# A linear-attention block with a feed-forward part on one core: w_ch1 in pieces of whole rows, one pair of half-rows instead of two, another order of the steps

## The chip, the cores and the metric

The kernel runs on one core of a Trainium2 chip. The metric is the device time of one execution in microseconds; lower is better. A core has five engines with queues of their own: TensorE (PE, with its weight loads as PEld), VectorE (DVE), ScalarE (ACT), GpSimd (POOL) and SyncE (SP, which here only issues DMAs). All wait for each other through semaphores.

## The reference

Two parts follow each other. The first is a recurrent linear attention for 4 batches, 8 heads, 768 tokens and 48 channels a head; the second is a layer norm and a two-layer feed-forward part with a residual.

```python
for t in range(S):                                  # S = 768, state is [B, H, 48, 48]
    cur = einsum('bhd,bhe->bhde', u[None] * kt, vt)
    y[:, :, t] = einsum('bhd,bhde->bhe', rt, state + cur)
    state = w[None, :, :, None] * state + einsum('bhd,bhe->bhde', kt, vt)
x = y.transpose(0, 2, 1, 3).reshape(B, S, 384)
xn = (x - mean(x)) / sqrt(var(x) + 1e-6) * g_ln
out = x + maximum(xn @ w_ch1, 0) @ w_ch2            # w_ch1 is 384 x 1536, w_ch2 is 1536 x 384
```

All inputs and the output are fp32.

## The kernel before, in words

The tokens are cut into 24 chunks of 128 (six for each batch). Two neighbouring chunks are one attention group, 12 in all. For the feed-forward part the chunks are grouped again by `GROUPS`: eight single chunks, six groups of two, four single ones.

Every step is a small function with a short name, and `PLAN` is a long list of entries "name,number,engine" that are issued in this order. `v`, `s` and `g` mean VectorE, ScalarE and GpSimd; `-` means that the step has only one engine (TensorE, or SyncE for a load or store). Nothing reorders the steps afterwards: each engine's queue holds its own steps in the order of the list. So PLAN fixes which engine does a product or a copy, and what stands behind what.

The steps that matter here:

- `LK`, `LR`, `LV` load k, r and v of one chunk; a packet is one head's row of 48 numbers. `LK2`, `LR2`, `LV2` load a pair of chunks so that a partition holds two neighbouring tokens, and a packet is 96 numbers. r is loaded as pairs for groups 0 to 8 in both versions. k and v are loaded as pairs only for the first `PAIRS` groups.
- `SKH`/`SK2`/`SK` and `SRH`/`SR2`/`SR` multiply k and r by powers of w into bf16 (`sk`, `sr`): a product of two tensors in on-chip memory. `CV2` casts v to bf16 (`vv`). `VB2` multiplies v by a number per head (`Vb`), `Q2` multiplies the transposed k and r, `ZD` scales the state.
- `TRk`/`TRr` transpose sk and sr on TensorE and `TCk`/`TCr` copy them out; from group 4 on sk (and from group 9 on sr) is transposed by a DMA instead (`TDk`, `TDr`).
- `AT`/`AM`, `S`/`ZU`, `Y`/`X` are the attention itself: scores and their mask, the state, the output with the v term. `AT2`, `AM2`, `Y2` are the same for chunks held as pairs.
- `XN`, `SQ`, `RS` are the norm; `LT`/`XT` (TensorE and a copy) or `LTD` (DMA) transpose its result.
- `LW1` loads a piece of w_ch1, `SW` scales one 128 x 512 block of it by g_ln into bf16, in blocks i = 3n + kc for columns n and rows kc; `IW2` loads a third of w_ch2 from GpSimd's queue. `UP` is a feed-forward block of the first layer, `RL` its relu, `DN` a third of the second layer of a chunk, `OT` scaling and residual, `STO` the store.
- `DU` issues matmuls of 512 columns on a tile of zeros, as often as its number divided by 512.

A w_ch1 piece before is a third of the columns of all rows, `w1_f[n]` (128 x 3 x 512, packets of 2 KB). The UP entry number is 16 times the group plus the block m, which for a single chunk covers columns n = m: UP,2 needs SW,6 to 8, UP,17 (group 1, m = 1) needs SW,3 to 5, UP,0 needs SW,0 to 2.

In traces several steps share one line, since a helper records them: products of two tensors have line 205, copies line 200 (ScalarE) or 202. They are told apart by their tiles.

## Time and profile before

| what | value |
|---|---|
| timed runs | 147.73, 149.15, 152.63 us (median 149.15) |
| profiled execution, span from first to last instruction | 147.5 us; what lies around the span is not on the page, and the fastest timed run is 0.2 us longer |
| busy PE, PEld, DVE, ACT, POOL | 141.5, 111.1, 112.3, 82.4, 72.0 us |
| granted TensorE clock | 1.000 |
| DMA | 27.18 MB in 85097 packets, 80338 of them under 512 B |
| loads of k, r, v (issue to landing) | 4.2 to 5.0 us |
| w_ch1, three pieces of 768 KB | 8.6 us |
| w_ch2, three pieces, issued by GpSimd | 6.0 us |

The page gives the busy time of each engine, the span in 40 slices with the busy share in tenths, the DMA queues, the chain of waits that ended last, and the costliest groups of instructions. A row of a timeline has start, duration, engine, line, operation, output and inputs, shapes and, in brackets, the idle time ahead of it with what ended it. A row of a table of waits has the sum, the number and the longest of them.

### The profile page before, as it was taken

The numbers are of one execution on the slowest core, as the hardware profiler recorded it, in microseconds if no ns is written. First come the engines' busy times: TensorE is split into PE (matmuls) and PEld (weight loads), VectorE is DVE, ScalarE is ACT, GpSimd is POOL, SyncE is SP. The second block draws the span as 40 slices with busy tenths as digits, with TensorE's granted clock in tenths as the row PEclk, the third lists the DMA queues.
The fourth block names the chain that finished last, engine by engine and source line by source line (L and its number), as shares of the span: only waits on it lengthen the run. The fifth ranks groups of instructions, "written<-read, shape, count | busy, mean of one in ns | idle before, by whom it ended". The sixth has DMA issues, their size and how long they took to land.

```text
span 147.5 us, 4689 instructions
## 1 busy us (share of the span) xinstructions
PE 141.5 (96%) x1943; PEld 111.1 (75%) x1943; DVE 112.3 (76%) x206; ACT 82.4 (56%) x181; POOL 72.0 (49%) x96
## 2 busy tenths in 40 slices
PE   7899999799999999999999999999999999999991
PEld 3375767699987788787778787778877777878881
DVE  3499999889559887998989999499644886851642
ACT  4657783986977737736766543115795164537010
POOL 7507687984070475794854194627129330614000
PEclk9999999999999999999999999999999999999999
DMA  4999997999959899999899997998959894213023
GB/s 112 300 242 240 192 339 187 283 243 215 220 95 231 202 225 165 264 205 258 164 192 196 195 235 124 173 204 227 197 112 191 182 142 154 82 46 119 8 99 111
DMA packets 85097, 27.18 MB, mean 184 GB/s; under 512 B 80338, under 2 KB 83540, under 8 KB 85076
## 3 DMA queue, kind: packets, MB, share of 16 engines
q1 hardware_dynamic: 84642, 25.70, 78.3%
q0 software_dynamic: 432, 1.18, 4.3%
q8 instruction: 15, 0.25, 0.7%
q14 instruction: 6, 0.05, 0.1%
q10 hardware_dynamic: 2, 0.00, 0.0%
HBM read 18.88 MB, written 4.72 MB: 160 GB/s over the span
## 4 chain that ended last, share of the span: by engine, by line
PE 65%; SPq 13%; DMA 11%; DVE 6%; POOL 1%; issue 1%; DVEq 0%
PE o L674 28%; PE hp L646 25%; DMA kf<-in_k_dram 6%; DMA w_f<-in_moe_w_ch_dram 5%; SPq L374 4%; SPq L352 3%; PE at L544 3%; PE y L583 2%; SPq L358 2%; PE y L481 2%; PE y L575 2%; SPq L371 1%; SPq L377 1%; DVE hT L664 1%; PE y L460 1%
## 5 line engine op out<-in xcount | busy, mean ns | idle before, releaser
L646 PE MATMUL hp<-xT,w_sb 128*128 128x128 bf16 (+1 forms) x648 | 57.1, 237 | 0.8 <-ACT w_sb L342 0.7
L662 ACT ACTIVATE hT<-hp 128x512 bf16<-128x512 f32 x55 | 32.4, 594 | 40.5 <-PE hp L646 39.7
L646 PEld LDWEIGHTS <-w_sb 128*128 128x128 bf16 x648 | 49.3, 114 | 5.1 <-ACT w_sb L342 1.3
L674 PE MATMUL o<-w_sb,hT 128*128 128x384 bf16 x276 | 53.0, 326 | 0.0
L674 PEld LDWEIGHTS <-hT 128*128 128x128 bf16 x276 | 25.0, 97 | 12.0
L553 DVE TENSOR_TENSOR A<-at,mask 128x1024 bf16<-128x1024 f32 x20 | 24.2, 1216 | 2.1 <-PE at L544 2.1
L492 POOL TENSOR_TENSOR Vb<-vf,cc 128x768 f32<-128x768 f32 x11 | 16.5, 1498 | 14.9 <-ACT cc L200 8.5
L730 DVE SCALAR_TENSOR_TENSOR ot<-o,rs,x 128x384 f32<-128x384 f32 x23 | 14.1, 615 | 12.3 <-PE o L674 7.0
L205 POOL TENSOR_TENSOR sk<-kf,Fk 128x384 bf16<-128x384 f32 x13 | 13.6, 1053 | 8.5 <-DMA kf<-in_k_dram 7.9
L597 ACT ACTIVATE sqj<-x,sm 128x384 bf16<-128x384 f32 x24 | 14.6, 609 | 2.2 <-DVE x L590 2.2
L205 POOL TENSOR_TENSOR Z<-ZS,WLZ 128x384 bf16<-128x384 f32 x8 | 8.0, 1002 | 15.4 <-DVE ZS L565 15.4
L590 DVE SCALAR_TENSOR_TENSOR x<-y,Vb 128x384 f32<-128x384 f32 x20 | 11.0, 552 | 4.5 <-PE y L583 4.1
L664 DVE TENSOR_SCALAR hT<-hp 128x512 bf16<-128x512 f32 x17 | 11.5, 684 | 3.4 <-PE hp L646 3.3
L279 PE MATMUL o<-warm 128*128 128x512 bf16 x33 | 11.3, 427 | 1.0 <-DVE warm L228 1.0
L200 ACT COPY trr<-at 128x512 bf16<-128x512 bf16 (+1 forms) x13 | 9.1, 764 | 4.4 <-PE at L400 4.4
L205 DVE TENSOR_TENSOR sr<-rf,Fr 128x768 bf16<-128x768 f32 (+1 forms) x11 | 9.5, 870 | 1.6 <-DMA rf<-in_r_dram 1.6
L205 POOL TENSOR_TENSOR sr<-rf,Fr 128x384 bf16<-128x384 f32 (+1 forms) x5 | 6.6, 1325 | 7.0 <-DMA rf<-in_r_dram 7.0
L604 ACT ACTIVATE xn<-x,sm 128x384 bf16<-128x384 f32 x13 | 7.8, 609 | 2.3 <-DVE x L590 2.3
L606 POOL TENSOR_SCALAR xn<-x,sm 128x384 bf16<-128x384 f32 x8 | 5.3, 665 | 7.6 <-DVE x L590 7.5
L205 DVE TENSOR_TENSOR q<-trk,trr 128x1024 bf16<-128x1024 bf16 x9 | 7.5, 837 | 1.4 <-ACT xn L604 1.0
L481 PE MATMUL y<-vv,sk 128*128 128x96 bf16 (+1 forms) x96 | 7.3, 204 | 0.3 <-ACT vv L200 0.2
L205 DVE TENSOR_TENSOR sk<-kf,Fk 128x384 bf16<-128x384 f32 (+1 forms) x10 | 7.4, 747 | 0.0
(97 smaller groups left out, 179.4 us busy)
## 6 DMA issues: line engine op xcount, KB each, us to landing
out_dram<-ot SPq DMA_DIRECT2D x23, 192.0 KB, 2.6
kf<-in_k_dram SPq DMA_DIRECT2D x20, 192.0 KB, 4.2
vf<-in_v_dram SPq DMA_DIRECT2D x20, 192.0 KB, 4.3
rf<-in_r_dram SPq DMA_DIRECT2D x9, 384.0 KB, 4.7
...
```

What stands on the lines that cost most here:

```text
L205: engines[e].tensor_tensor(out=out, in0=in0, in1=in1, op=ALU.mult)
L279: nc.tensor.matmul(out=warm_ps[0][:].rearrange("p (a t) -> p a t", a=4), lhsT=warm[:], rhs=rhs, start=True, stop=True)
L481: nc.tensor.matmul(out=t[:, q * E2 : (q + 1) * E2].rearrange("p (e d) -> p e d", e=2), lhsT=lhs, rhs=rhs, start=first, stop=True, skip_gro ...
L492: engines[e].tensor_tensor(out=Vb2(g).rearrange("p (x h d) -> p x h d", x=2, h=H), in0=vals, in1=cc2(g)[:].unsqueeze(3).to_broadcast([P, 2 ...
L553: nc.vector.tensor_tensor(out=AA(i)[:].rearrange("p e q t -> p (e q) t"), in0=psum["at", i][:].rearrange("p e q t -> p (e q) t"), in1=mask ...
L590: nc.vector.scalar_tensor_tensor(out=xx(i)[:], in0=psum["y", i][:, :C], scalar=1.0, in1=Vb(i), op0=ALU.mult, op1=ALU.add, accum_out=sm[i][:],)
L597: nc.scalar.activation(out=sqj[:], in_=xx(i)[:], func=ACT.Square, bias=sm[i][:], scale=-float(C), accum_out=sq[g][:, j : j + 1])
L646: nc.tensor.matmul(out=t[:, a * gw : (a + 1) * gw], lhsT=w1_sb[n][kc][:, fb::FB], rhs=xT(g)[:, :size, kc, :], start=(kc == 0), stop=(kc == ...
L662: nc.scalar.activation(out=o, in_=s, func=ACT.Relu)
L664: nc.vector.tensor_relu(out=o, in_=s)
L674: nc.tensor.matmul(out=psum["o", i][:, :C], lhsT=hT(g)[:, fk, j * P : (j + 1) * P], rhs=w2_sb[d][:, a, :], start=(fk == 0), stop=(fk == FK ...
L730: nc.vector.scalar_tensor_tensor(out=ot(i)[:], in0=psum["o", i][:, :C], scalar=rs[g][:, j : j + 1], in1=xx(i)[:], op0=ALU.mult, op1=ALU.add,)
```

## The change

Four things change. `LW1` loads whole rows: `w1_f[kc]` holds 128 rows of w_ch1 with all 1536 columns (packets of 6 KB), so that the three pieces are cut by rows and each UP needs all three. `PAIRS` goes from 2 to 1, so that group 1 loads k and v as four single chunks (`LK`, `LV` instead of `LK2`, `LV2`) and uses AT, AM, Y instead of AT2, AM2, Y2. On GpSimd `CV2` is a product with two constants instead of a copy. And PLAN is another list: the order differs all through it, and so does the engine of many steps.

```diff
-PAIRS = 2
+PAIRS = 1
 PLAN = """
...
-S,3,- LW1,0,- TCk,2,s DU,512,- SK,6,v LT,1,- Y2,2,- SQ,0,s SW,5,g XT,1,v SW,3,s LV,6,- LT,0,- SW,4,v TRk,3,- Q2,2,g
...
+X,3,v LT,1,- Y,2,- SW,3,s SQ,1,s LK,7,- LK,6,- XT,0,v XT,1,v X,2,v SW,5,v SW,2,v AT,4,- TRr,3,- S,3,- UP,17,- TCr,3,s RL,17,s
...
 """
...
-    w1_f = [const.tile([P, CK, FW], FP32, name=f"w1_f{n}") for n in range(NW)]
+    w1_f = [const.tile([P, F], FP32, name=f"w1_f{kc}") for kc in range(CK)]
...
-    w1_src = moe_w_ch1.rearrange("(kc p) (n f) -> p n kc f", p=P, n=NW)
+    w1_src = moe_w_ch1.rearrange("(kc p) f -> p kc f", p=P)
...
-    def LW1(n, e):
-        nc.sync.dma_start(out=w1_f[n][:], in_=w1_src[:, n])
+    def LW1(kc, e):
+        nc.sync.dma_start(out=w1_f[kc][:], in_=w1_src[:, kc])
...
-        o, s = w1_sb[n][kc][:], w1_f[n][:, kc]
+        o, s = w1_sb[n][kc][:], w1_f[kc][:, n * FW : (n + 1) * FW]
...
     def CV2(g, e):
-        copy(e, vv2(g), vf2(g))
+        if e == "g":
+            nc.gpsimd.tensor_scalar(
+                out=vv2(g), in0=vf2(g), scalar1=1.0, scalar2=1.0, op0=ALU.mult, op1=ALU.mult
+            )
+        else:
+            copy(e, vv2(g), vf2(g))
```

Counted over PLAN, GpSimd gets SK 17 (before 13), SR2 5 (2), SR 4 (3), Q2 4 (3), SW 4 (1), CV2 5 (3), XN 9 (8), RS 9 (8), one SKH and one SRH (0), and fewer VB2, 7 (11), and ZD, 5 (8). VectorE gets VB2 5 (1), ZD 7 (4), XN 6 (3), RL 18 (17) and fewer SK 5 (7, and one SK2), SR2 3 (6), SR 2 (3), SKH and SRH 1 each (2 each), Q2 8 (9), CV2 3 (4), XT 6 (8). ScalarE gets fewer SW, 3 (6), XN, 9 (13), CV2, 4 (5) and RS, 9 (10). The number of zero-tile matmuls stays at 33.

The first place is SyncE's queue between the loads of group 0 and the last piece of w_ch1. The tiles w_f_223 to w_f_225 are the pieces 0 to 2, kf, rf and vf the loaded k, r and v; rf_76 is the r of group 3. Before:

```order
L374 DMA rf_75<-in_r_dram 128x8x96
L352 DMA kf_71<-in_k_dram 128x8x48
L374 DMA rf_76<-in_r_dram 128x8x96
L377 DMA vf_78<-in_v_dram 128x8x96
L352 DMA kf_71<-in_k_dram 128x8x48
L352 DMA kf_72<-in_k_dram 128x8x48 x2
L335 DMA w_f_224<-in_moe_w_ch_dram 128x3x512
L335 DMA w_f_225<-in_moe_w_ch_dram 128x3x512
L358 DMA vf_79<-in_v_dram 128x8x48 x2
L335 DMA w_f_223<-in_moe_w_ch_dram 128x3x512
```

And in the changed kernel:

```order
L376 DMA vf_77<-in_v_dram 128x8x96
L357 DMA vf_78<-in_v_dram 128x8x48 x2
L373 DMA rf_75<-in_r_dram 128x8x96
L334 DMA w_f_224<-in_moe_w_ch_dram 128x1536
L351 DMA kf_71<-in_k_dram 128x8x48
L334 DMA w_f_223<-in_moe_w_ch_dram 128x1536
L373 DMA rf_76<-in_r_dram 128x8x96
L334 DMA w_f_225<-in_moe_w_ch_dram 128x1536
L357 DMA vf_79<-in_v_dram 128x8x48 x2
```

The pieces of w_ch1 moved ahead of the k of chunks 5 to 7 and of the v of group 2 (vf_79); the r of group 3 (rf_76) moved from ahead of all pieces to between the second and the third.

The second place is GpSimd's queue from the products of the first groups to the last load of w_ch2. A tile w_sb_a_b is a scaled block of w_ch1, w_sb_235 to w_sb_237 the thirds of w_ch2; xn is the centred x. Before:

```order
L205 TENSOR_TENSOR sr_87<-rf_75,Fr_209 128x16x48
L492 TENSOR_TENSOR Vb_112<-vf_77,cc_102 128x768
L205 TENSOR_TENSOR sk_84<-kf_71,Fk 128x8x48 x2
L205 TENSOR_TENSOR sk_82<-kf_72,Fk 128x8x48
L606 TENSOR_SCALAR xn_126<-x_114,sm_141 128x384
L492 TENSOR_TENSOR Vb_113<-vf_78,cc_103 128x768
L346 TENSOR_SCALAR w_sb_2_231<-w_f_224,g_neg 128x512
L205 TENSOR_TENSOR q_97<-trk_93,trr_96 128x1024
L606 TENSOR_SCALAR xn_128<-x_116,sm_143 128x384
L349 DMA w_sb_235<-in_moe_w_ch_dram 128x1536
```

And in the changed kernel, from the Q2 of group 1 on:

```order
L204 TENSOR_TENSOR q_98<-trk_92,trr_95 128x1024
L204 TENSOR_TENSOR sk_84<-kf_71,Fk 128x8x48
L348 DMA w_sb_235<-in_moe_w_ch_dram 128x1536
L610 TENSOR_SCALAR xn_127<-x_115,sm_142 128x384
L204 TENSOR_TENSOR sr_85<-rf_76,Fr_209 128x16x48
L348 DMA w_sb_236<-in_moe_w_ch_dram 128x1536
L345 TENSOR_SCALAR w_sb_1_227<-w_f_224,g_neg 128x512
L345 TENSOR_SCALAR w_sb_0_226<-w_f_223,g_neg 128x512
L348 DMA w_sb_237<-in_moe_w_ch_dram 128x1536
L345 TENSOR_SCALAR w_sb_1_233<-w_f_224,g_neg 128x512
L345 TENSOR_SCALAR w_sb_2_234<-w_f_225,g_neg 128x512
```

The first load of w_ch2 moved ahead of the scalings of w_ch1; the product of group 3's r (sr_85 from rf_76), which VectorE did before, stands ahead of two scalings that UP,0 reads (w_sb_1_227 and w_sb_0_226).

More of the change, by code (lines that the diff above doesn't have):

```diff
@@ L66 @@
-SB,23,- OA,23,v SA,23,-
+WF,0,s TL,0,s ML,0,v LN,0,s MI2,0,g MM,0,g MP,5,g MO,0,v MZ,0,v MP,2,g MP,0,g MM2,0,g MI,0,g MP,4,g MP,1,g MW,0,v DU,3072,-
+WBM,0,- LK2,0,- FK2,1,s FK2,0,s SKH,0,g SKH,1,v LR2,0,- LK,2,- UF,0,- LG,0,- LK,4,- UWR,0,v LR2,1,- LK,3,- LV2,0,- LV,2,- LV,3,-
+LR2,2,- LW1,1,- LK,5,- LW1,0,- LR2,3,- LW1,2,- LV,5,- LV,4,- FR2,1,s FR2,0,s SRH,1,g DU,4608,- TRk,0,- DU,512,- SRH,0,v TCk,0,s
+FK,0,s FR,0,s SR2,1,g SK,3,g MP,3,g TRr,0,- COL,0,- TCr,0,v Q2,0,v UW,0,s CV2,0,g WL,0,s AT2,1,- AT2,0,- DU,3072,- AM2,1,v
@@ new lines @@
+AM2,0,v SK,4,g SK,2,v TRr,1,- S,0,- DU,1536,- TRk,1,- CV2,1,s TCr,1,s TCk,1,s ZU,0,v CC2,0,v VB2,0,g SR2,2,v S,1,- Q2,1,g SK,5,g
+Y2,0,- AT,2,- Y2,1,- TRr,2,- ZU,1,v AM,2,v TCr,2,s X,1,v X,0,v IW2,0,g XN,1,g SR2,3,g IW2,1,g XN,0,s AT,3,- DU,512,- AM,3,v
+S,2,- DU,512,- ZU,2,v CC2,1,s UGC,0,s SW,4,s TRk,2,- DU,1024,- LT,0,- Y,3,- DU,512,- TCk,2,s SW,1,g SW,0,g DU,1536,- VB2,1,v
+X,3,v LT,1,- Y,2,- SW,3,s SQ,1,s LK,7,- LK,6,- XT,0,v XT,1,v X,2,v SW,5,v SW,2,v AT,4,- TRr,3,- S,3,- UP,17,- TCr,3,s RL,17,s
@@ new lines @@
+IW2,2,g UP,0,- AT,5,- UP,1,- Q2,2,v ZU,3,v CV2,2,v AM,5,v RL,0,s SW,6,s UP,16,- S,4,- RL,1,s SQ,2,s SW,7,g SW,8,g XN,2,g UP,2,-
+LT,2,- CC2,2,v ZU,4,v RL,16,s SQ,0,s XN,3,s UP,18,- DN,0,- VB2,2,g XT,2,v RL,2,v RL,18,s LT,3,- AM,4,v UP,34,- Y,5,- X,5,v
+XT,3,v SK,7,g SK,6,g DN,1,- UP,32,- Y,4,- TRk,3,- DN,2,- RS,0,g X,4,v OT,0,v LK,8,- LV,6,- LV,7,- RS,1,g XN,4,g SK,8,v RL,34,s
+TCk,3,s LR2,4,- LK,11,- LK,9,- LV,9,- LR2,5,- SK,9,g LV,8,- LK,10,- TDk,4,- LR2,6,- LV,12,- UP,33,- SQ,3,s AT,6,- AT,7,- CV2,3,s
```

81 lines of the change are left out of this document (35 added, 46 removed).

## The prediction, made before the changed kernel was run

> **What bounds the kernel now.** I read the page's engine line and slices first, then TensorE's own waits, then the start of its long stretch, then the transfers that this start waits for.
>
> ```profile
> PE 141.5 (96%) x1943; PEld 111.1 (75%) x1943; DVE 112.3 (76%) x206; ACT 82.4 (56%) x181; POOL 72.0 (49%) x96
> PE   7899999799999999999999999999999999999991
> ```
>
> TensorE is busy for 96% of the span, VectorE for 76%, GpSimd for 49%. "Busy" says little of the first 27 us, where the program itself issues matmuls on a zero tile (line 279) to fill gaps. So the next question is where the real work becomes dense.
>
> ```profile
> 25.12 0.62 PE L544 MATMUL at<-trr,trk 48*128 48x128 bf16 x16
> 26.10 0.25 PE L646 MATMUL hp<-xT,w_sb 128*128 128x128 bf16 x1
> 26.71 0.25 PE L646 MATMUL hp<-xT,w_sb 128*128 128x128 bf16 x1 [0.37 <-ACT w_sb L342]
> 27.33 1.42 PE L646 MATMUL hp<-xT,w_sb 128*128 128x128 bf16 x22 [0.36 <-ACT w_sb L342]
> 143.74 0.67 PE o L689 x8
> ```
>
> The feed-forward matmuls (UP, line 646) begin at 26.10 and run without a gap from 27.33; the last DN piece ends at 144.4. What waits remain on TensorE in between is the whole answer for 27.4 to 147 us:
>
> ```profile
> PE hp L646 <- ACT w_sb L342: 0.4, 1, 0.4
> PEld L544 <- issue: 1.7, 6, 0.3
> PEld L646 <- ACT w_sb L342: 0.5, 1, 0.5
> PEld L481 <- DVE x L590: 0.5, 1, 0.5
> PEld L646 <- issue: 0.3, 1, 0.3
> PEld L400 <- DVE sr L205: 0.3, 1, 0.3
> ```
>
> The two w_sb rows are the edge of the start. "issue" is no wait for another engine. Only 0.5 + 0.3 us are waits for VectorE. So behind 27.33 lie 117 us in which a better order of VectorE and GpSimd can give back at most 0.8 us, or about 1.5 with some of "issue"; it can lose any amount. What decides is **when the UP stream begins**, and that start waits for w_ch1:
>
> ```profile
> 15.90 7.37 DMA w_f<-in_moe_w_ch_dram
> 19.38 1.00 POOL L205 TENSOR_TENSOR sk<-kf,Fk 128x384 bf16<-128x384 f32 x1 [0.56 <-DMA kf<-in_k_dram]
> 19.57 5.58 SPq L335 DMA_DIRECT2D w_f<-in_moe_w_ch_dram  x1
> 25.32 1.95 ACT L342 ACTIVATE w_sb<-w_f,g_neg 128x512 bf16<-128x512 f32 x3 [1.31 <-DMA w_f<-in_moe_w_ch_dram]
> 2.00:4.00 2.00, 2.00 (x6) 0.93 (x4) 0.14 (x4) 1.06 (x2) 1.82 (x11) 1.00 0.98 249
> 20.00:22.00 2.00, 2.00 (x30) 1.35 (x28) 2.00 (x3) 1.56 (x4) 1.90 (x3) 1.00 1.01 377
> 24.00:26.00 2.00, 2.00 (x59) 1.35 (x57) 2.00 (x6) 0.69 (x3) 2.00 (x2) 1.00 0.48 74
> ```
>
> The first w_ch1 piece lands at 15.90 + 7.37 = 23.3, the second at 25.3 (ACT then scales three blocks, the third of which ends at 27.27 and releases the stream). The third piece sits 5.58 us in SyncE's issue. In the stretch rows the last two numbers are the DMA share and GB/s: the engines are full from 2 us on and half empty at 24 to 26, behind that stuck issue.
>
> **The change part by part.**
>
> *Loads and w_ch1.* Prices first. The last k load before w_ch1 lands at 19.38, so twelve loads (eight pairs of half-rows, four single chunks) took 17.3 us of full engines from 2.0.
>
> ```profile
> DMA packets 2193, 0.55 MB, mean 184 GB/s; under 512 B 2118, under 2 KB 2118, under 8 KB 2193
> q1 hardware_dynamic: 2193, 0.55, 93.4%
> q0 software_dynamic: 432, 1.18, 4.3%
> ```
>
> The first two rows are the stretch 16 to 19, with single chunks of 1024 packets (128 x 8) in it: 0.934 x 3 = 2.80 us, less 0.41 for 75 packets of w_ch1 (0.154 MB at 377 GB/s), is 2.39 us for 2118 packets, so 1.16 us a chunk. A pair is then (17.3 - 4 x 1.16)/8 = 1.58 us. Splitting group 1's k and v from two pairs into four chunks costs 4.64 - 3.16 = 1.5 us of DMA time. A w_ch1 piece is 0.786 MB: 2.1 us at 377 GB/s, or 2.4 (19.3 to 25.3 held two pieces and one v chunk: (6.0 - 1.16)/2). Pieces of whole rows are as large; I take the same 2.1 to 2.4, since the 377 GB/s stretch is the fastest that I see.
>
> In the new order six pairs and six chunks go before the last w_ch1 piece: 2.0 + 6 x 1.58 + 6 x 1.16 + 3 x (2.1 to 2.4) = 24.7 to 25.6. Before GpSimd reaches the head's end it also issues the first w_ch2 load (IW2,0), which was issued at 27.03 and now stands behind SK,5, at about 21 us; the three w_ch2 loads took 4.3% of 147.5, 2.1 us each, so up to 2.1 more: 24.7 to 27.7, taken at 26.5. The 5.58 us in SyncE should mostly go, since three pieces are 384 packets instead of 1152; what is late next is the transfers themselves. Every piece is now needed by every UP, where the old start needed two of three; that eats what the earlier issue wins.
>
> The row with which a rule can be weighed is 377 GB/s with 2 KB rows. The Trainium skill, "DMA: Bandwidth & Descriptors", Specifications, puts the least transfer at line rate at 512 B; by that rule 2 KB and 6 KB rows cost the same and whole rows bring nothing. The trace agrees as far as it goes: by the rule the sum is 24.7 to 25.6 before w_ch2, as above, and no row here shows 6 KB.
>
> *GpSimd's queue before the first UPs.* The r load of group 3 (LR2,3) now stands behind two w_ch1 pieces; it lands one piece before the last, 22.6 to 23.2, up to 25.3 with w_ch2 between, taken at 24.0. GpSimd, in order, waits for it in SR2,3, and behind it stand IW2,1 and the two scalings SW,1 and SW,0, without which UP,0 cannot start.
>
> ```profile
> 12.15 1.81 POOL L205 TENSOR_TENSOR sr<-rf,Fr 128x768 bf16<-128x768 f32 x1 [6.44 <-DMA rf<-in_r_dram]
> 23.37 0.49 DVE L344 TENSOR_SCALAR w_sb<-w_f,g_neg 128x512 bf16<-128x512 f32 x1 [0.18 <-DMA w_f<-in_moe_w_ch_dram]
> 23.44 0.97 POOL L346 TENSOR_SCALAR w_sb<-w_f,g_neg 128x512 bf16<-128x512 f32 x1 [0.94 <-DMA w_f<-in_moe_w_ch_dram]
> 27.03 0.78 POOL L349 DMA_DIRECT2D w_sb<-in_moe_w_ch_dram  x1
> ```
>
> 24.0 + 1.81 + 0.78 + 2 x 0.97 = 28.5 for SW,0 (26.9 to 29.8). UP,17 needs only SW,3, 4 and 5: 26.5 + 0.49 = 27.0, so it runs alone and TensorE then waits for SW,0. Dense work starts at 28.5 instead of 27.33: **+1.2**. Not yet done then, but done in the kernel before: one transpose of sk (TRk,3) and one AT, 0.45 and 0.55 by the rows below: **+1.0**. Done ahead: UP,17, **-0.7**. Two zero-tile matmuls that stood behind 27.33 are gone, 0.2 each: **-0.4**. Sum +1.1.
>
> ```profile
> 28.75 0.38 PE L279 MATMUL o<-warm 128*128 128x512 bf16 x1
> 28.97 0.83 PE L646 MATMUL hp<-xT,w_sb 128*128 128x128 bf16 x12
> 55.71 0.45 PE at L400 x8
> 61.78 0.55 PE at L544 x16
> ```
>
> *Group 1 as single chunks.* AT2 and Y2 on two half-rows become AT and Y. All of it lies before the stream, under the wait for w_ch1, so I cost it at nothing. So too the zeroing of the warm tile, now last of VectorE's memsets (some 1.2 us later), and the halves of SK and SR shared with GpSimd: by the old durations the state of group 0 is some 2 us later, and the first transposed x stands at about 24, with 2.5 us of cover until w_ch1. If that cover goes (w_ch1 at 24.7), up to 0.7 us shows.
>
> *VectorE and GpSimd.* GpSimd gets four SK, one SR, SKH and SRH more (1.0 each, as sk at 19.38), three SR2 and a Q2 (1.8 each), three SW (1.0) and two CV2 (1.3, below), and gives back four VB2 (1.5) and three ZD (about a product of 384, 1.0): 7 + 7.2 + 3 + 2.6 - 9 = 10.8, and 1.4 more as its three old CV2 become slower. So 72 becomes about 84 us. VectorE, which has the other side of most of these, comes out some us lower. Products that coincide do stretch each other:
>
> ```profile
> 21.03 1.48 POOL L492 TENSOR_TENSOR Vb<-vf,cc 128x768 f32<-128x768 f32 x1
> 21.33 1.59 DVE L205 TENSOR_TENSOR sk<-kf,Fk 128x384 bf16<-128x384 f32 x1
> 35.60 0.59 DVE L205 TENSOR_TENSOR sk<-kf,Fk 128x384 bf16<-128x384 f32 x1
> 36.12 0.94 DVE L205 TENSOR_TENSOR sr<-rf,Fr 128x768 bf16<-128x768 f32 x1
> L205 DVE TENSOR_TENSOR sk<-kf,Fk 128x384 bf16<-128x384 f32 x9 | 6.4, 724 | 0.0
> L205 DVE TENSOR_TENSOR sr<-rf,Fr 128x768 bf16<-128x768 f32 x6 | 6.8, 1136 | 0.3 <-DMA rf<-in_r_dram 0.3
> L202 POOL CAST vv<-vf 128x768 bf16<-128x768 f32 x3 | 2.5, 825 | 0.0
> ```
>
> Beside a product on GpSimd the same VectorE product takes 1.59 instead of 0.59 us. But over nine sk (724 against 590) that is 1.2 us, over six sr (1136 against 940 free) 1.2: a few us in all on an engine that is idle for 35, under TensorE's dense stream. Worth at most the 0.8 us of waits above; I take **-0.5**. A GpSimd copy written as a two-factor product (CV2) isn't in the trace; by bounds it lies between the cast's 0.83 us and 1.48, what SW's 0.97 for 512 elements makes for 768; I take 1.3, nearer to SW, which is the same instruction. GpSimd's idle half covers it, but for the one in the head, CV2,0, whose 0.5 us lies under the wait for w_ch1 too.
>
> GpSimd takes 1.81 us for an sr of 768 where VectorE takes 0.94 free. The Trainium skill, "GPSIMD Engine Reference", Engine selection, says to leave two-input products to VectorE, as GpSimd is about twice as slow. The trace agrees (1.9 times). By that rule SR2,3 would be better left on VectorE, and SW,0 would end near 27.6 instead of 28.5.
>
> Sum: +1.1 - 0.5 = **+0.6 us**: 148.1 for the profiled span of 147.5. The three timed runs have 147.73, 149.15 and 152.63, so the profile stands with the fastest; on the median 149.15 the forecast is **149.7**.
>
> **The rivals.**
>
> *Faster: transfers share instead of queueing.* If LR2,3 overtakes the w_ch1 pieces ahead of it and lands by 21.4, SW,0 ends at 25.9; if the last piece lands at 24.7 too, UP,17 starts at 25.2 and the stream follows at once, with nothing of it done ahead: -2.1 + 1.0 - 0.4 = -1.5, and the waits give -0.8 to -1.5 more: -2.3 to -3.0, 146.5 on the median. For it: the order of the program puts SR2,3 well ahead of SW. Against it: the engines are full, so what lands early makes another piece late.
>
> *Slower: GpSimd's backlog reaches SyncE.* SyncE's queue is in order and already waits for GpSimd:
>
> ```profile
> SPq L423 <- POOL rs L616: 4.2, 1, 4.2
> SPq L423 <- POOL sk L205: 2.0, 2, 1.1
> ```
>
> A transposing load (line 423) that waits for a late sk holds all k, v, r loads behind it. With SR2,3 at 25.3, SW,0 ends at 29.8 (+1.3 on the forecast); if the backlog, with 12 us more work on GpSimd, is not worked off before the sk of group 4 is due, one such hold of 2 to 4 us comes through to TensorE: +0.6 + 1.3 + 2 = +3.9, 153.0. It decides once GpSimd is later than TensorE's need of sk; behind SW,0 GpSimd has 6.9 us to the end of SK,6 (an issue 0.8, two SW, an xn 0.6, a Vb 1.5, two sk), TensorE some 8 us to TRk,3 (nine pieces of UP, DN and AT at 0.6, the rest small), so there is about 1 us of slack, and none if the k loads behind w_ch1 are late.
>
> *Nothing changes:* w_ch1 comes as before, the stretches go elsewhere, TensorE covers both: 149.2. It lies within the forecast's own range.
>
> **How the numbers follow.** Forecast with the null 0.60, own range 147.5 to 151.5; faster rival 0.19, slower rival 0.21. The range takes in most of both: 146.0 to 153.0. Two per cent, about what can be told from no change here, is 3 us. The faster rival only just reaches it, so faster 0.16, within 0.62, slower 0.22.
>
> **What would show it.** Right: UP,17 alone near 27, then a TensorE wait for w_sb by GpSimd, dense from about 28.5; SR2,3 idle until about 24 for r; the long SyncE issue of w_ch1 gone; VectorE's sk near 600 ns; GpSimd near 84 us. Wrong: dense from 25 (the faster rival), or TensorE waits of 2 us and more after 40 us (the slower one).

## The result, and the profile after

The changed kernel takes 156.26 us (median of four runs, 155.72 to 157.22) beside 150.89 us of the kernel before on the same chip. The ratio is **1.0549, 95% interval 1.0467 to 1.0631**: slower by 5 to 6%, and outside the forecast's range. The profiled execution took 156.56 us with a span of 154.8 us, 7.3 us more than the span before. (Ratios compare fast executions alone: two of the four behind the 150.89 us, 152.63 and 153.61 us, are slow ones, the profiles of only_singles and new_head_old_rest below are of slow ones too, and pool_short and new_head_old_rest have too few fast ones for a ratio.)

First the page after: the busy line, TensorE's slices and the granted clock.

```profile
PE 141.8 (92%) x1863; PEld 111.1 (72%) x1863; DVE 115.3 (74%) x201; ACT 79.7 (51%) x176; POOL 86.6 (56%) x108
PE   4979994999968999989999999999999999999991
PEclk9999998699999999999999999999999999999999
```

TensorE is busy as long as before (141.8 against 141.5 us) in a span that is 7.3 us longer. So nothing was added to its work; it waits. A slice is 3.9 us: there is a 4 at 23 to 27 us, a 6 and an 8 at 43 to 50, an 8 at 66 to 70, and the clock falls to 8 and 6 tenths at 23 to 31 us.

The views of stretches put numbers to it. Columns: length of the stretch, busy time and instructions of PE, PEld, DVE, ACT and POOL, then the granted clock. First before, then after.

```profile
24.00:28.00 4.00, 3.23 (x73) 2.25 (x72) 4.00 (x9) 2.47 (x5) 3.97 (x5) 1.00 0.67 178
28.00:32.00 4.00, 4.00 (x86) 3.64 (x84) 2.90 (x6) 3.89 (x7) 3.31 (x2) 1.00 1.16 254
32.00:140.00 108.00, 107.86 (x1389) 87.63 (x1386) 84.33 (x153) 59.38 (x142) 51.22 (x59) 1.00 0.84 174
```

```profile
24.00:28.00 4.00, 2.08 (x28) 1.69 (x28) 3.54 (x8) 1.17 (x3) 3.89 (x6) 0.76 1.10 204
28.00:32.00 4.00, 4.00 (x61) 3.64 (x59) 4.00 (x6) 3.20 (x6) 1.42 (x3) 0.82 1.09 201
32.00:140.00 108.00, 104.34 (x1365) 84.40 (x1363) 88.38 (x155) 57.48 (x134) 60.11 (x61) 1.00 0.81 166
```

From 32 to 140 us TensorE idles 108.00 - 104.34 = 3.7 us, against 0.1 before. This row, "idle from 32 to 140", is the yardstick of the experiments. In 28 to 32 it is busy all the time at a clock of 0.82, which loses 0.18 x 4 = 0.7 us of work.

TensorE's timeline gives the start of the dense UP stream and the wait ahead of it; the rows of VectorE and GpSimd give the reason.

```profile
26.25 0.48 PE L579 MATMUL y<-Z,trr 128*128 128x96 bf16 x4 [1.92 <-DVE x L594]
29.00 1.73 PE L650 MATMUL hp<-xT,w_sb 128*128 128x128 bf16 x24
22.23 3.30 DVE L496 TENSOR_TENSOR Vb<-vf,cc 128x768 f32<-128x768 f32 x1 [0.24 <-ACT cc L199]
25.63 0.56 DVE L594 SCALAR_TENSOR_TENSOR x<-y,Vb 128x384 f32<-128x384 f32 x1
22.26 0.59 POOL L610 TENSOR_SCALAR xn<-x,sm 128x384 bf16<-128x384 f32 x1
22.82 1.81 POOL L204 TENSOR_TENSOR sr<-rf,Fr 128x768 bf16<-128x768 f32 x1
25.23 1.53 POOL L345 TENSOR_SCALAR w_sb<-w_f,g_neg 128x512 bf16<-128x512 f32 x2
DMA to landing us min/median/max: 7.0/8.5/9.2
```

The stream is dense at 29.00 instead of 27.33 (+1.7). VB2,1, a product of 768 elements that VectorE does in 0.94 us when left alone (the kernel before has one at 37.45), takes 3.30 us: GpSimd's xn and sr lie over it, and it ends 0.9 us after sr does (22.82 + 1.81 + 0.9 = 25.53). Behind it stands X,3, which frees the one buffer "y" that TensorE writes into (in PSUM); Y,2 on TensorE waits 1.92 us for that. The last row is that of w_ch1's issues: the third piece, issued at 14.88, is there by 24.1 at the latest.

Then the two longest stalls of the rest. TensorE first, then what it waited for on ScalarE and on SyncE.

```profile
46.91 0.83 PE L650 MATMUL hp<-xT,w_sb 128*128 128x128 bf16 x12 [1.88 <-ACT hT L666]
45.69 0.17 ACT L199 COPY cc<-y 128x16 f32<-128x16 f32 x1 [2.13 <-DVE Z L204]
68.87 0.84 PE L650 MATMUL hp<-xT,w_sb 128*128 128x256 bf16 x6 [0.50 <-DMA xT<-xn]
SPq L427 <- POOL vv L394: 7.7, 1, 7.7
61.09 2.42 POOL L204 TENSOR_TENSOR sk<-kf,Fk 128x384 bf16<-128x384 f32 x2
55.74 1.48 POOL L496 TENSOR_TENSOR Vb<-vf,cc 128x768 f32<-128x768 f32 x1 [4.71 <-DVE cc L201]
```

At 45 us ScalarE stands 2.13 us in the copy CC2,3 (released when VectorE has done ZU,6), and the relu that TensorE needs stands behind it in ScalarE's queue. Up to 63.5 us SyncE is held at a transposing load, 7.7 us by the view of waits (its issue before that ends at 56.9), until GpSimd has made the two sk of 61.09 (the row names vv, the step behind them); GpSimd itself had stood 4.71 us in VB2,4.

The sum: +1.7 (start), +0.7 (clock), +3.5 (idle from 32 to 140) are 5.9 of the 7.3 us. The other 1.4 is by subtraction; the forecast's 1.0 us of work not yet done when the stream starts fits into it.

The clock's share is larger than that 0.7, since the work between the gap and the stream ran slowly too. In the run cc_on_dve below, whose list is the same up to the stream, the gap is there but the clock of the profiled execution stays at 1.00:

```profile
PEclk9999999999999999999999999999999999999998
26.39 0.33 PE L574 MATMUL y<-Z,trr 128*128 128x96 bf16 x4 [1.79 <-DVE x L589]
27.98 1.58 PE L645 MATMUL hp<-xT,w_sb 128*128 128x128 bf16 x24
```

From Y,2 to the stream it takes 27.98 - 26.39 = 1.6 us; in the changed kernel's profile it was 29.00 - 26.25 = 2.75. So some 1.2 of the +1.7 are the clock's as well, an estimate from these two profiles, and the clock's part of the 7.3 us is about 1.9.

### The profile page after: what moved, and what is told of

It is laid out like the page before. It is cut to its first block, busy times and chain, and to the rows that moved or that the text cites. A ratio compares the mean times of both kernels' runs of the same rounds, so it can differ in the third digit from the quotient of the medians.

```text
span 154.8 us, 4538 instructions
## 1 busy us (share of the span) xinstructions
PE 141.8 (92%) x1863; PEld 111.1 (72%) x1863; DVE 115.3 (74%) x201; ACT 79.7 (51%) x176; POOL 86.6 (56%) x108
## 3 DMA queue, kind: packets, MB, share of 16 engines
q0 software_dynamic: 432, 1.18, 4.4%
## 4 chain that ended last, share of the span: by engine, by line
PE 49%; POOL 18%; DVE 12%; issue 11%; DMA 5%; ACT 2%; SPq 0%; POOLq 0%; DVEq 0%; ACTq 0%
PE hp L650 18%; PE o L678 18%; POOL sr L204 4%; POOL sk L204 3%; POOL q L204 3%; DMA xT<-xn 3%; DVE A L557 2%; PE at L404 2%; DVE Vb L496 2%; DMA vf<-in_v_dram 2%; PE y L587 2%; PE at L548 2%; PE y L579 2%; DVE Z L204 2%; DVE A L529 2%
## 5 line engine op out<-in xcount | busy, mean ns | idle before, releaser
L557 DVE TENSOR_TENSOR A<-at,mask 128x1024 bf16<-128x1024 f32 x22 | 26.6, 1215 | 0.6 <-PE at L548 0.6
L204 POOL TENSOR_TENSOR sk<-kf,Fk 128x384 bf16<-128x384 f32 x18 | 19.8, 1110 | 5.9 <-DMA kf<-in_k_dram 4.0
L496 POOL TENSOR_TENSOR Vb<-vf,cc 128x768 f32<-128x768 f32 x7 | 11.4, 1624 | 19.1 <-ACT cc L199 7.8
L204 POOL TENSOR_TENSOR sr<-rf,Fr 128x384 bf16<-128x384 f32 (+1 forms) x10 | 14.3, 1440 | 0.1
L199 ACT COPY trr<-at 128x512 bf16<-128x512 bf16 x14 | 9.4, 740 | 7.9 <-PE at L404 7.9
L204 POOL TENSOR_TENSOR Z<-ZS,WLZ 128x384 bf16<-128x384 f32 x5 | 5.4, 1072 | 9.4 <-DVE ZS L569 9.4
L204 POOL TENSOR_TENSOR q<-trk,trr 128x1024 bf16<-128x1024 bf16 x4 | 8.8, 2205 | 2.4 <-DMA trr<-sr 2.4
L569 DVE TENSOR_TENSOR ZS<-y,Z 128x384 f32<-128x384 f32 x12 | 6.6, 552 | 4.0 <-PE y L485 2.6
L620 POOL TENSOR_SCALAR rs<-sq 128x1 f32<-128x1 f32 (+1 forms) x9 | 3.0, 338 | 11.4 <-ACT sqj L601 10.9
L204 DVE TENSOR_TENSOR sk<-kf,Fk 128x384 bf16<-128x384 f32 x6 | 5.4, 902 | 4.5 <-ACT Fk L300 4.5
```

The lines of the kernel that those rows point to most:

```text
L199: nc.scalar.copy(out=out, in_=in_)
L204: engines[e].tensor_tensor(out=out, in0=in0, in1=in1, op=ALU.mult)
L496: engines[e].tensor_tensor(out=Vb2(g).rearrange("p (x h d) -> p x h d", x=2, h=H), in0=vals, in1=cc2(g)[:].unsqueeze(3).to_broadcast([P, 2 ...
L557: nc.vector.tensor_tensor(out=AA(i)[:].rearrange("p e q t -> p (e q) t"), in0=psum["at", i][:].rearrange("p e q t -> p (e q) t"), in1=mask ...
```

## The experiments

Five batches, each with runs of the kernel before on the same chip. Moves in PLAN are shown as diffs of its entries.

### Which part of the change costs: order, engines, pieces, singles

**old_order** keeps the list and engines of before, and takes the other three parts.

```diff
-PLAN of the change
+PLAN of before, with LK,2 LK,3 for LK2,1 (and so on) and LW1,0 right behind LW1,2
```

> The order and engines of the kernel before, with the three other parts of the change (w_ch1 in row pieces, the third piece issued right behind the second; group 1 as single chunks; GpSimd's v cast as a product with constants). Theory O (the new list of steps costs the 7 us): within 2 us of the kernel before, span 146 to 149.5. Theory P (row pieces, single chunks or the cast cost them): span above 152.

152.84 us, ratio **1.0267 (1.0176 to 1.0358)**. TensorE:

```profile
24.82 0.34 PE L575 MATMUL y<-Z,trr 128*128 128x96 bf16 x4 [2.44 <-DVE Z L200]
30.22 1.42 PE L646 MATMUL hp<-xT,w_sb 128*128 128x128 bf16 x22 [0.37 <-ACT w_sb L337]
32.00:140.00 108.00, 107.91 (x1417) 87.98 (x1415) 85.14 (x154) 62.33 (x147) 54.01 (x60) 1.00 0.87 175
```

A wait of 2.44 us at a Y, dense at 30.22, and idle from 32 to 140 of 0.1 us as before. So these parts lose 2.7% in the old order, and none of it as idle time behind 32 us (part of the loss at the start is a lower clock, 0.93 in 28 to 32). The 3.7 us behind 32 us come only with the new list.

**new_order_old_engines** has the new order, with every step on its old engine.

```diff
-VB2,1,v SR2,3,g XN,1,g ...
+VB2,1,g SR2,3,v XN,1,s ...
```

> The order of the changed kernel, but every step on the engine that it had before; the other parts as changed. Theory G (more products on GpSimd collide with VectorE's and hold them up): most of the loss goes, 147.5 to 150.5. Theory Q (the order alone, what stands behind what in the in-order queues): 152 and more, however few products GpSimd has.

177.62 us, 1.1923 (1.1835 to 1.201). GpSimd's old share does not bring the time back: the new order does not suit the old engines, 26 us worse than the kernel before. For the same reason the run can't say what GpSimd's extra work costs in the list that was made for it; the opposite, the old order on the new engines, was not run.

**new_head_old_rest** and **old_head_new_rest** splice the two lists at the first UP.

```diff
-PLAN of one list
+its entries up to the first UP, then the entries of the other that are still missing, in the other's order
```

> Up to the first UP the list of the changed kernel, from there the list before (steps already done left out); other parts as changed. Theory H (one collision in the head, VectorE's Vb beside GpSimd's sr, with the clock that it costs): nearly all of the loss stays, 152 to 155. If the loss is spread, the head's share is +1.7 for the start of UP and +0.7 for the clock: 149.5 to 151.

> Up to the first UP the list before, from there that of the changed kernel; other parts as changed. Theory H: near the kernel before, 147 to 149. If the loss is spread, the waits of TensorE behind 30 us stay, 4.7 us in the changed kernel's trace: 151 to 153.5, and the stalls at 45 us (ScalarE's relu behind a copy that waits for VectorE) and at 68 us (a late transposing load) are seen again.

The first took 159.0 us; the splice itself made a wait of 7.0 us for an sk, up to 33 us, so it says nothing of the head. The second took 159.28 us, 1.0667 (1.0569 to 1.0766), a span of 156.6 us where 151 to 153.5 was expected, with the stalls of the changed kernel at its rest:

```profile
32.00:140.00 108.00, 103.71 (x1353) 83.96 (x1351) 86.98 (x152) 56.06 (x130) 58.49 (x60) 1.00 0.83 169
```

4.3 us of idle with the old head, with 1.93 us for a relu at 48.8 and 0.37 us for an xT at 70.7 as in the changed kernel. The stream starts late here too, but so it does in old_order, which idles 0.1 us: the waits behind 32 us belong to the new list's rest and are not handed down by a late start.

**only_singles** and **only_rows** are the kernel before with one part each.

```diff
-PAIRS = 2
+PAIRS = 1
```

> The kernel before with one thing changed: group 1's k and v as single chunks (so AT, AM, Y instead of the pair forms), w_ch1 by columns and the order as before. Theory S (Y shares the one PSUM buffer named y with the state matmuls, while Y2 had the two hp buffers, so TensorE waits there for VectorE): the wait of 2.4 us at 22 to 25 us seen in old_order comes back and UP starts at 29 to 30 instead of 27.3; span 149 to 150.5. Theory D (old_order's loss is the row pieces, all three needed by the first UP): span within 1 us of the 147.5 before.

```diff
-w1_f[n]: 512 columns of all rows; LW1,0 behind S,3
+w1_f[kc]: 128 whole rows; LW1,0 behind LW1,2
```

> The kernel before with one thing changed: w_ch1 in pieces of rows, with the third piece issued right behind the second. Theory S: UP starts within 1 us of 27.3, span 146.5 to 148.5. Theory D: the last of three pieces lands 2 us after the second column piece did, UP starts at 29 or later, span 149 to 150.5.

Singles: 1.0254 (0.997 to 1.0537), which alone can't be told from no change. Rows: 1.0275 (1.0184 to 1.0365). First singles, then rows:

```profile
24.98 0.50 PE L570 MATMUL y<-Z,trr 128*128 128x96 bf16 x4 [2.64 <-DVE Z L200]
27.61 0.25 PE L640 MATMUL hp<-xT,w_sb 128*128 128x128 bf16 x1 [1.31 <-ACT w_sb L336]
28.84 1.90 PE L640 MATMUL hp<-xT,w_sb 128*128 128x128 bf16 x22 [0.37 <-ACT w_sb L336]
```

Each delays the start by itself: singles by a wait at Y (as in old_order, 2.44 us), rows by 1.5 us because every UP now needs all three pieces. Together they cost no more than one (old_order, 1.0267), since both delay the same start.

**y_on_hp** asks why singles wait: the kernel before with singles, but with the Y of chunks 2 and 3 in the two buffers that Y2 used.

```diff
-        t = psum["y", i] = ps.tile([P, 512], FP32, name="y")
+        t = psum["y", i] = ps_h.tile([P, 512], FP32, name="hp") if i in (2, 3) else ps.tile([P, 512], FP32, name="y")
```

> The kernel before with group 1 as single chunks, but with the Y of chunks 2 and 3 in the two PSUM buffers that the Y2 of the pairs used, instead of the single buffer that S and Y share. The buffer theory: what the singles cost in the old order (1.0254 on the time, a wait of 2.64 us for Z at the Y of chunk 3) came from that shared buffer; then Y no longer stands in a wait of over 1 us, the feed-forward stream is dense near 27.5 us and the ratio is 0.995 to 1.012 (TensorE's own work in AT and Y of singles is about 0.2 us away from that of pairs). The rival, that the singles' longer loads (1.5 us more of DMA time) set the delay: waits stay, now for chunk data or for w_sb, dense near 28.3, ratio 1.015 to 1.03.

1.0147 (1.0086 to 1.0207). The 2.64 us wait is gone and the stream is dense at 27.74:

```profile
27.74 1.42 PE L641 MATMUL hp<-xT,w_sb 128*128 128x128 bf16 x22 [0.37 <-ACT w_sb L337]
```

So the wait was the shared buffer's: Y2 had the two "hp" buffers, Y shares one with S. What is left of the ratio lies between the two expectations; the start alone (+0.4 us) does not account for it, and its cause stays open.

### Mending single waits of the changed kernel

**vb_on_pool** takes VectorE's VB2,1 out of GpSimd's way.

```diff
-XN,1,g SR2,3,g IW2,1,g XN,0,s ... CC2,1,s ... VB2,1,v
+XN,1,g XN,0,s ... CC2,1,s VB2,1,g SR2,3,g IW2,1,g
```

> The changed kernel with one collision taken out: VB2,1 goes from VectorE to GpSimd, and GpSimd's SR2,3 and IW2,1 go right behind it. Theory H (this collision holds X,3, with it the y buffer, Y,2 and the scaling of w_ch1, and lets the TensorE clock fall): the wait of 1.9 us at 24.3 and the fall of the clock go, UP starts at 27 to 28, span 152 to 153.3. If X,3 waits as long for Vb on GpSimd, or SW,0 behind SR2,3 takes its place, 154 to 155.5.

157.07 us, 1.0556 (1.0466 to 1.0646): nothing gained.

```profile
25.45 0.33 PE L630 MATMUL at<-ident,xn 128*128 128x128 bf16 x3 [1.53 <-DVE xT L196]
29.01 1.58 PE L645 MATMUL hp<-xT,w_sb 128*128 128x128 bf16 x22 [1.54 <-DVE w_sb L338]
```

The wait of 1.92 us is gone, and two others of 1.5 us stand in its place; dense at 29.01, as before the edit. VectorE now waits 2.21 us for that Vb of GpSimd, and its two scalings of w_ch1, which the second row waits for, take 3.12 us beside GpSimd's sr and scalings (1.31 us in cc_on_dve): the collision is not gone, it has moved.

**cc_on_dve** takes the copy that ScalarE stood in at 45 us to VectorE, right behind what it waits for.

```diff
-ZU,6,v UP,49,- DN,6,- XT,4,s CC2,3,s
+ZU,6,v CC2,3,v UP,49,- DN,6,- XT,4,s
```

> The changed kernel with CC2,3 on VectorE right behind ZU,6 instead of on ScalarE, where it stands ahead of a relu that frees an hp buffer. Theory Q (waits in the in-order queues): the wait of 1.9 us at 45 goes and 1 to 2 us of the span with it, 152.9 to 154. If TensorE would wait there for VectorE's other work anyway (theory G), no change, 154.3 to 155.3.

153.89 us, **1.0375 (1.024 to 1.0509)** instead of 1.0549. The wait at 45 us is gone, and idle from 32 to 140 falls from 3.7 to 2.5 us:

```profile
32.00:140.00 108.00, 105.53 (x1372) 85.32 (x1371) 88.66 (x157) 57.16 (x132) 61.08 (x62) 1.00 0.81 169
```

That one is an in-order wait, shown, and by the rows it is worth 1.2 us. The time fell by 2.4 us, more than that, because the clock stayed up in most of its executions: three with a mean granted clock of 0.997 to 1.00 took 153.36 to 153.97 us, and one at 0.989 took 155.45, beside 155.72 to 157.22 for the changed kernel, whose four executions were all at 0.989.

**sk_early** is cc_on_dve with, in addition, an earlier place for the sk that SyncE waited for.

```diff
-VB2,4,g X,8,v OT,3,v ZD,8,g ... SK,12,g ... SK,13,g
+SK,12,g SK,13,g VB2,4,g X,8,v OT,3,v ZD,8,g ...
```

> The changed kernel with CC2,3 on VectorE (as in cc_on_dve) and, new, with the k products of chunks 12 and 13 on GpSimd ahead of VB2,4, in a place where GpSimd stood idle for 4.7 us. The theory of SyncE's queue: the transposing load of sk of group 6 held SyncE for 7.7 us there and starved the transfers, which is why an xT came late for UP near 66 to 69 us; then SyncE's wait for sk falls below 3 us, the wait of 0.5 us for xT at 65 to 69 us goes, some of the small waits behind it too, and the time falls by 0.5 to 1.5 us against cc_on_dve: ratio 1.027 to 1.034. The rival, that the transfers there are late by the order of the loads themselves: SyncE waits less, but TensorE's waits stay and the ratio is 1.036 to 1.04.

155.12 us, 1.0428 (1.0375 to 1.0481). SyncE issues the transposing load at 55.10 instead of 60.23 in cc_on_dve (63.5 in the changed kernel), the wait for xT at 66 to 69 us is gone, another of 0.6 us stands at 53, and idle falls by 0.4 us against cc_on_dve:

```profile
55.10 3.80 SPq L422 DMA_TRANSPOSE trk<-sk  x1
32.00:140.00 108.00, 105.89 (x1378) 85.46 (x1376) 89.46 (x157) 57.87 (x135) 61.12 (x62) 1.00 0.79 168
```

The time did not fall and lies above both expected ranges: the lower clock was back in three of the four executions (0.987 to 0.989). The wait is real and worth some tenths of a microsecond, less than the runs can tell.

**two_mends** is cc_on_dve with the edit of y_on_hp, **mended** has both and sk_early's too.

> The changed kernel with CC2,3 on VectorE and the Y of chunks 2 and 3 in the PSUM buffers of Y2, without the earlier k products, which in the kernel with three mendings pushed a Z on GpSimd back and made a new wait of 1.7 us at 54.7 us. If the mendings add up: the stream starts at 27.4 us as there, no wait of over 1 us behind 30 us, ratio 1.02 to 1.03. If each mending only moves the wait to the next step of the list: a wait of 1 us or more appears elsewhere, ratio 1.03 to 1.04.

> The changed kernel with three mendings: CC2,3 on VectorE, the k products of chunks 12 and 13 earlier, and the Y of chunks 2 and 3 in the two PSUM buffers of Y2. If the 1.8 us wait of Y for X just before the stream is the shared buffer's, the stream starts 1.0 to 1.8 us earlier than in sk_early (27.2 to 28 us instead of 29) and the ratio is 1.015 to 1.022. If VectorE's queue (Vb stretched to 3.3 us beside GpSimd) sets the start, xT of the first chunks comes no earlier: dense at 28.5 to 29, another wait (for xT or w_sb by VectorE) in its place, ratio within 0.004 of sk_early.

two_mends: 153.7 us, 1.0264 (1.0145 to 1.0383). mended: 153.77 us, 1.0336 (1.0239 to 1.0434), between its two expectations. In mended TensorE and GpSimd show

```profile
27.38 1.76 PE L645 MATMUL hp<-xT,w_sb 128*128 128x128 bf16 x24
56.34 0.33 PE L574 MATMUL y<-Z,trr 128*128 128x96 bf16 x4 [1.44 <-POOL Z L199]
52.90 1.00 POOL L199 TENSOR_TENSOR sk<-kf,Fk 128x384 bf16<-128x384 f32 x1 [1.39 <-DMA kf<-in_k_dram]
```

The stream is dense at 27.38, as in the kernel before, 0.6 us ahead of cc_on_dve at the same clock; but 0.4 us of that were won ahead of it (VB2,1 starts at 22.10 instead of 22.50), so the shared buffer was worth some 0.2 us here. A gap of 1.7 us is still there, now for an xT of VectorE, behind a VB2,1 of 3.16 us. And the sk that were moved ahead now wait for their k loads, a Z behind them comes late, and TensorE stands 1.44 us. A mending made its own stall.

### GpSimd's length, the holding of VectorE, or the list

**pool_short** cuts GpSimd's two-operand products to an eighth; **pool_quiet** does that too, but fills the output twice with a constant first, so that GpSimd is as busy (89.4 us, against 86.6). Vb goes through the same helper there (line 212 instead of 496).

```diff
-        engines[e].tensor_tensor(out=out, in0=in0, in1=in1, op=ALU.mult)
+        if e == "g":
+            for _ in range(fills):  # pool_quiet: 2; pool_short: 0, or 1 in the first groups
+                nc.gpsimd.memset(out, 0.5)
+            out, in0, in1 = part(out), part(in0), part(in1)
+        engines[e].tensor_tensor(out=out, in0=in0, in1=in1, op=ALU.mult)
```

> The changed kernel with every two-operand product on GpSimd (sk, sr, q, Z, Vb) cut to an eighth of its elements; in the first groups, where a buffer is used for the first time, the rest is filled with a constant. Left out: seven eighths of these products. Order, engines, loads and waits stay. If the stalls after 30 us (6.2 us of gaps on TensorE against 1.5 before) come from GpSimd's products, because they hold VectorE up or are late themselves, the gaps fall to about 2 us, VectorE's sk, Z and Vb go to their free times (590, 540, 940 ns) and the span falls by 4 to 6 us, ratio 1.01 to 1.025. If the order of the list itself makes the stalls (a step in an engine's queue behind one that waits for TensorE), they stay at 4 us and more and the ratio is 1.035 or higher.

> As pool_short, but ahead of each cut product GpSimd fills its output twice with a constant, so that it is busy about as long as with the whole product (0.9 to 2 us) and reads little. Left out: seven eighths of the products. If what hurts is that two engines' products stretch each other, VectorE's times go to their free ones here too and the result is that of pool_short, within 1 us. If what hurts is that GpSimd's results are late, the stalls stay as in the changed kernel, 4 us and more after 30 us, ratio 1.04 to 1.055.

pool_short: 154.34 us beside 150.11; span 152.2, 2.6 us less than the changed kernel's. pool_quiet: 156.35 us, 1.0429 (1.0311 to 1.0548), span 154.6. VectorE's Vb by shape in the changed kernel, in pool_short and in pool_quiet (busy, mean ns):

```profile
L496 DVE TENSOR_TENSOR Vb<-vf,cc 128x768 f32<-128x768 f32 x5 | 7.9, 1581 | 0.2 <-ACT cc L199 0.2
L212 DVE TENSOR_TENSOR Vb<-vf,cc 128x768 f32<-128x768 f32 x5 | 4.8, 969 | 0.2 <-ACT cc L199 0.2
L212 DVE TENSOR_TENSOR Vb<-vf,cc 128x768 f32<-128x768 f32 x5 | 4.8, 968 | 0.2 <-ACT cc L199 0.2
```

VectorE's products are free of GpSimd in both. TensorE, pool_short first (start, a wait, idle from 32 to 140), then pool_quiet:

```profile
24.91 1.58 PE L658 MATMUL hp<-xT,w_sb 128*128 128x128 bf16 x22 [0.21 <-DVE w_sb L351]
31.02 0.38 PE L493 MATMUL y<-vv,sk 128*128 128x96 bf16 x4 [2.38 <-DVE vv L201]
32.00:140.00 108.00, 105.77 (x1366) 86.31 (x1364) 86.09 (x157) 55.33 (x129) 27.22 (x63) 0.99 0.82 169
25.01 0.34 PE L643 MATMUL at<-ident,xn 128*128 128x128 bf16 x3 [2.09 <-POOL xn L618]
28.51 2.15 PE L658 MATMUL hp<-xT,w_sb 128*128 128x128 bf16 x24
32.00:140.00 108.00, 104.00 (x1365) 84.38 (x1363) 85.99 (x156) 57.57 (x134) 62.81 (x131) 1.00 0.82 167
```

With a short GpSimd the stream starts **4.1 us earlier** (1.2 of them the clock's, by the estimate above), and yet only 2.6 us of span are won: TensorE then stands 2.38 us for a v and still idles 2.2 us behind 32. So GpSimd's products, by their length or by what they hold up, do set the start; and more than half of the idle time behind 32 us stays when GpSimd is busy for 27 us of that stretch instead of 60, as the list's own.

pool_quiet was to tell length from holding, and does not. It starts at 28.51 and idles 4.0 us, much like the changed kernel, but for another reason:

```profile
21.51 0.96 DVE L212 TENSOR_TENSOR Vb<-vf,cc 128x768 f32<-128x768 f32 x1 [0.24 <-ACT cc L199]
23.53 0.78 POOL L356 DMA_DIRECT2D w_sb<-in_moe_w_ch_dram  x1 [2.93 <-issue]
```

VB2,1 is short here, and X,3 done by 23.1 us. TensorE waits 2.09 us for an xn instead, which GpSimd begins at 24.36 (22.26 in the changed kernel), because it pauses for 2.93 us ahead of issuing a w_ch2 load. The profile names nothing that it waits for, and the changed kernel has no such pause. Behind 32 us two waits for GpSimd's q and Z, 0.80 and 0.58 us, are new, with GpSimd 2.7 us busier in that stretch. So the run shows that VectorE's products run free beside fills; what their stretching costs the changed kernel stays open.

### The clock, the pieces, and the start itself

**filled** puts eight zero-tile matmuls into the gap of 1.9 us.

```diff
-X,3,v LT,1,- Y,2,-
+X,3,v LT,1,- DU,4096,- Y,2,-
```

> The changed kernel with eight zero-tile matmuls of 512 columns (1.7 us) ahead of the Y of chunk 2, in the gap of 1.9 us before the dense stretch. Theory that a gap costs twice, by itself and by the lower granted clock behind it (0.76 for 24 to 28 us and 0.82 for 28 to 32): the clock stays at 0.98 or more up to 40 us and the time falls by 1 to 1.7 us, ratio 1.043 to 1.048, though the gap is as long. Theory that the dip has another cause (the load of the start itself): the clock falls as before and the ratio stays at 1.053 to 1.058.

154.94 us, 1.0342 (1.0219 to 1.0465), more gained than either expectation had it; span 152.7.

```profile
24.00:28.00 4.00, 3.63 (x41) 2.11 (x40) 3.81 (x8) 2.07 (x4) 3.89 (x6) 1.00 1.11 205
28.00:32.00 4.00, 4.00 (x76) 3.63 (x74) 3.86 (x6) 3.72 (x7) 3.18 (x3) 1.00 1.11 212
```

The clock is 1.00 where it was 0.76 and 0.82, and the span is 2.1 us shorter. But it is also 1.00 in the profiled execution of cc_on_dve, which has the gap and no filling. The dip comes in some executions of a kernel and not in others: mean granted clock 0.989 in all four of the changed kernel, in one of four of filled, and in one of four of cc_on_dve. So the runs show what a dip costs (two_mends: 155.12 us at 0.988, 153.14 to 154.14 us at 1.00), and not that filling the gap prevents it.

**cols_mended** takes the suspected causes at the start away together: columns again, the edits of two_mends, and the filling (here ahead of AT,4, where two_mends waits 1.68 us).

> The changed kernel with w_ch1 in pieces of columns again, CC2,3 on VectorE, the Y of chunks 2 and 3 in the buffers of Y2, and eight zero-tile matmuls ahead of AT of chunk 4, in the gap of 1.9 us that two_mends still had there. What is left of the change is the new list with its engines, and group 1 as single chunks. If the head's three shown causes and the clock are most of the loss: from 1.0264 (two_mends) by 0.7 to 1.5 us for the clock and 0 to 1 us for the pieces to 1.01 to 1.02. The list's own waits behind 30 us (4.6 us of gaps against 1.5) should stay, so it should not reach before: a ratio below 1.005 would say that these waits cost nothing. If the pieces matter in this order as they did in the old one, the stream starts by 27 us; if VectorE and GpSimd set the start, at 27.5 to 28.5 us as with rows.

153.03 us, 1.0275 (1.0204 to 1.0347): a miss, expected was 1.01 to 1.02.

```profile
27.77 1.77 PE L645 MATMUL hp<-xT,w_sb 128*128 128x128 bf16 x24
32.00:140.00 108.00, 106.03 (x1378) 85.98 (x1376) 88.45 (x157) 57.78 (x135) 61.52 (x62) 1.00 0.84 171
```

Dense at 27.77 (+0.4), full clock, but 2.0 us idle from 32 to 140: with 1.0 us of work not yet done that is most of the 3.6 us by which its span (151.1) exceeds that of before. Nothing here tells whole rows from columns in the new list.

**w1_first** and **w1_first2** ask of the kernel before whether its start hangs on w_ch1: the loads of w_ch1 go ahead of k and r of group 3. In w1_first the transpose of group 3's r was put ahead of the product that it should transpose, so it reads what the buffer held; its trace only tells when the UPs begin. The products and transposes of group 3 also move behind the first UPs, which the diff leaves out, and one zero-tile matmul is gone.

```diff
-LR2,3,- ... LK,6,- ... LK,7,- LW1,1,- ... LW1,2,- LV,5,- ... LV,4,- ... LW1,0,-
+LW1,1,- ... LW1,2,- LK,6,- LK,7,- LW1,0,- LR2,3,- LV,5,- ... LV,4,-
```

> The kernel before (columns, two pairs) with the loads of w_ch1 ahead of k and r of group 3, the products and transposes of that group behind the first UPs, and one zero-tile matmul less. If w_ch1's transfers set the start of the dense stretch, as the forecast read the profile of before, about 3.9 us of loads fewer ahead of them bring UP,2 from 26.1 to 24 to 24.8 us and the dense stretch from 27.33 to 25 to 25.5; 0.9 us of transposes are then still to be done, so the end comes 0.8 to 1.5 us earlier, ratio 0.99 to 0.995. If the start is set by the chain through Y, X and xT, UP,2 comes near 25.5 to 26 and the ratio is 0.997 to 1.01.

> The kernel before with the loads of w_ch1 ahead of k and r of group 3, and the products and transposes of that group behind UP,17 and S,4, each behind what it reads. In w1_first, which stood in a wait of 1.4 us for a free PSUM buffer at its transpose of sr, the UPs themselves began at 24.7 instead of 26.1 us. If that start can be kept, the stream is dense from 24.7 to 25.5 us, with 0.9 us of transposes and 0.5 us less of zero-tile matmuls on the other side: ratio 0.985 to 0.995. If the waits for the late k and r of group 3 come after all (transposes, then scores of chunks 6 and 7), TensorE stands 1 us or more between 27 and 34 us and the ratio is 1.0 to 1.015.

w1_first: 1.0274 (1.0195 to 1.0354), UPs from 24.70. w1_first2: 151.83 us, 1.0188 (1.0098 to 1.0277). Both are slower than either of their expectations.

```profile
25.33 1.50 PE L640 MATMUL hp<-xT,w_sb 128*128 128x128 bf16 x24
29.34 0.61 PE L394 MATMUL at<-ident,sk 128*128 128x128 bf16 x8 [1.18 <-DVE A L547]
```

In w1_first2 24 UP matmuls in a row start at 25.33, 2.0 us before the dense stretch of the kernel before, and TensorE then stands 1.18 us in a transpose that needs a PSUM buffer which VectorE frees late. The start can be moved by the transfers; the end came later. No version beat the kernel before.

## Why the prediction was wrong, step by step

**What bounds the kernel.** TensorE, and the start of the UP stream: right as far as it goes, and not enough. "It can lose any amount" behind 27.33 stood there as an aside; 3.5 us were lost there, the largest term, and the sum had -0.5 for it. (That the profile "stands with the fastest" run is a misreading: wherever a run's time and span are both on record, the time is 1.7 to 1.9 us longer, so the span of 147.5 goes with the median of 149.15. The forecast of 149.7 does not hang on it.)

**Loads and w_ch1.** 24.7 to 27.7 us, taken at 26.5, for the last piece; it was there by 24.1, below the range. The long issue on SyncE is gone as forecast (5.58 us, now 2.99 at most). "That eats what the earlier issue wins" was too mild: rows alone cost 1.0275 in the old order.

**GpSimd's queue before the first UPs.** The step failed. r was not late: SR2,3 began at 22.82 without a wait (24.0 forecast), the scalings ended at 25.23 + 1.53 = 26.8 (28.5), and TensorE waited for no w_sb of GpSimd. UP,17 did not run alone at 27. The stream started at 29.00 for another reason; that +1.2 was near +1.7 is chance. The rule weighed there, two-input products left to VectorE (the Trainium skill, "GPSIMD Engine Reference", Engine selection), may have been on the right track: with all of GpSimd's products cut short the stream starts at 24.9. No run gave only SR2,3 back to VectorE.

**Group 1 as single chunks, costed at nothing.** Failed: "under the wait for w_ch1" was the cover, and w_ch1 came before it was needed. Singles alone made a wait of 2.64 us, by the one PSUM buffer; the forecast counted loads and matmuls of the singles and no buffers. In the new list that buffer was worth only some 0.2 us of the start (mended); there VectorE's late VB2,1 stands behind the gap.

**VectorE and GpSimd, -0.5.** The step that failed and cost most: 0.5 us were to be won under TensorE's dense stream, and 3.5 us were lost there. GpSimd's 84 us were right (86.6), and CV2's product was over-sized (1.3; measured 0.93). Two things were wrong. The price of a coincidence was taken from averages and one row of 1.59 us; VB2,1 took 3.30 us, since two instructions of GpSimd followed each other. And "under TensorE's dense stream" took the density of the old order for a property of the kernel: each queue is in order, and a step that waits holds up those behind it that TensorE needs (CC2,3 at 45 us, 1.9 us). VectorE's sk did not go to 600 ns but to 902. The wait at 45 us is shown by its removal (idle 3.7 to 2.5 us in cc_on_dve); that the rest is the new list's follows from old_order and old_head_new_rest, but not wait by wait. Whether the stretching itself was rightly priced low stays open: pool_quiet, free of it, was no faster, but its GpSimd was later.

**The clock** was no term of the sum at all. With the dip that followed the gap of 1.9 us at the start it cost about 1.9 us, 0.7 of them behind the start of the stream.

**The rivals.** The slower one named a mechanism that is there: GpSimd late, SyncE held at a transposing load (7.7 us), more waits of TensorE after 40 us. But the longest of these, 1.88 us, came by ScalarE's queue and not by SyncE's. The hold was priced at 2 us for one hold and came out at some tenths; many waits of other kinds made up the rest, so that 153.0 too was short of 156.3. The faster rival's premise, loads that come earlier, came true (the last piece of w_ch1 by 24.1 us, r by 22.8) and won nothing.
